# A fused attention, routed-expert and dense-layer kernel: the routed loop ahead of the last tile, the dense layer's operands in another order, its weights loaded four steps ahead

## The chip, the cores and the metric

One core of a Trainium2 chip runs the whole program. The metric is the device time of one execution in microseconds (us); the median over several executions counts. Engines are called by the names of the profile: PE multiplies matrices, DVE and ACT do elementwise work, POOL does elementwise work and the indexed transfers, SP issues nearly all other DMAs. Each engine takes its own instructions in the order in which the program lists them.

## What is computed

```python
attn_out = _attn_ref(q, k, v)            # windowed attention, 4 x 8 heads, 576 positions
x = attn_out.transpose(0, 2, 1, 3).reshape(2304, 512)
# routed experts: 8 experts, one for each token
h = np.maximum(x[mask] @ w1[e], 0.0)     # 512 -> 1024
out[mask] = gate_w[mask, None] * (h @ w2[e])
# dense layer, on all 2304 tokens
h = x @ w_in                             # 512 -> 2048
r = np.maximum(h, 0.0)
return ((r * r) @ w_out)                 # 2048 -> 512
```

## The kernel before

**Stages.** Attention fills the first 130 us or so. The tokens are then gathered by expert into five slots of up to 512 tokens (`NSLOT`, the last one of 384, `SHORT`), each with one expert: first the way up (8 products `ffn1`), then the way down, one tile of 128 tokens after the other (`ffn2`, 24 matrix products each). `put` copies a tile's result out of PSUM (L718) and `scatter` writes its rows to `yd` with an indexed DMA on POOL (L724). A loop (`tc.For_i`, L1100) takes further chunks of 128 tokens, as many as the routing asks for at run time; with these inputs its body does not run once. Then the dense layer takes the 2304 tokens in three blocks (`NB`) and four passes (`PASSES`), each pass with a quarter of the hidden width.

**Precision.** Every fp32 operand is held as a high part and a low part; ACT writes the high part (a cast), DVE or POOL subtracts it from the operand for the low part, and a product is three matrix products (`passes`, L688).

**The dense layer.** One pass on one block is a visit; there are twelve (`visits`). `way_up` has seven steps, n = 0 to 6, of two halves q with six matrix products each, by a scheme that multiplies sums and differences of quarter matrices: weights a11, s1, s2, a12, s3, s4, a22 against tokens b11, t1, t2, b21, t3, b22, t4. In steps 0 to 2 ACT copies each half out of PSUM (L1213); in steps 3 to 5 DVE adds the copy to the new half (L1216) and squares it (L1192), ACT casts (L1184) and POOL subtracts (L1185). Steps 0, 2, 4 and 6 use the same PSUM banks (tag s), so step 4 waits for the copies of step 2, and step 6 for the adds of step 4. `way_down` then makes six tiles. `prepare(j)` makes the seven token operands of a block: a difference (L1155, DVE), the high part (L1170, ACT), the low part (L1171; POOL for b21 and b22 of the later blocks, else DVE), and a store to `xs` for later passes. For the first block it runs within the first visit, for the others within the way down before.

**The dense weights.** They arrive as 64-bit floats. `conv` turns half a chunk into fp32 on ACT (L635), DVE (L636 to L639) and POOL (L640), and stores it to `wc` (L641); `conv_load` (L628) loads it. There are 32 such halves; `conv_pace` spreads them over all five slots. `weights(p)` makes the operands of pass p from `wc`: two loads (L783), seven splits (L788 on ACT, L789 on DVE), four sums (`both`, L794 on DVE), then two more chunks (L826, L827). It is a generator; each `tick()` advances it by one step. Pass 0's runs in the last slot, those of passes 1 to 3 in the last visit of the pass before.

**The end of the routed part.** The last tile of the last slot is not scattered and read back: its result `yhl` is added into the first block with a 0/1 matrix `hot` (L1063), in eight groups of products (L1296 and L688), while the other rows of the block are read from `yd` by `yload(0)` (L1011).

```python
for f in range(8):
    ffn2(ps, hs[f][0][:, c], hs[f][1][:, c], W[s, 4 + f // 2], f, f == 0, f == 7)
    ...
conv_step(len(convs) + 1)
flush(0)
while bg:
    tick()
...
with tc.For_i(4 * (NSLOT - 1), total, 1) as ci:
```

Of the kernel before, what the change touches and what calls it, by code (L numbers as in the profile page):

```python
# [52 lines left out]
def attention_moe_kernel(ctx, tc, qh, kh, v, mid, wg, mb, w1, w2, win, wout, out):  # L53
# [711 lines left out]
    nconv = [0]  # L765

    def conv_step(upto):
        while nconv[0] < upto:
            if nconv[0]:
                conv(*convs[nconv[0] - 1])  # L770
            if nconv[0] < len(convs):
# [8 lines left out]
    def weights(p):  # L780
# [23 lines left out]
        split("s1", s1)  # L804
        yield
        s2 = both(s1, a11, ALU.subtract)
        yield
        split("s2", s2)
        yield
        split("a12", a12)  # L810
        yield
        s3 = both(a11, a21, ALU.subtract)
# [3 lines left out]
        s4 = both(a12, s2, ALU.subtract)  # L816
        yield
        split("s4", s4)
        yield
        split("a22", a22)  # L820
        yield
        for i in range(2):
            r = load(2 * p + 8 + i)
            yield
            h, l = wt("left", F32R), wt("left", F32R)
            act.copy(h, r)  # L826
            dve.tensor_tensor(l, r, h.bitcast(F32), op=ALU.subtract)  # L827
            dw[p]["o", i] = h, l
            yield
# [190 lines left out]
    for s in range(NSLOT):  # L1020
        n, nn = (SHORT if i == NSLOT - 1 else SLOT for i in (s, s + 1))
        nxt = s + 1 < NSLOT
        for f in range(8 if s else 0):
# [14 lines left out]
            if not nxt:  # L1038
                tick()
# [14 lines left out]
        for i in range(n // 128):  # L1054
            advance_load(8 * s + 4 + i + LA + 1)
            c = slice(128 * i, 128 * i + 128)
            ps = bank("t")
            if not nxt and i == n // 128 - 1:
                ids, hot = sm.tile([128, 1], F32, tag="ids", name="ids", bufs=1), wt("left", F32R)
                dve.tensor_copy(ids, xr[s][0][:, i:i + 1])  # L1060
                dve.tensor_tensor(ids, ids, again, op=ALU.add)
                for k_ in range(BT):
                    dve.tensor_scalar(hot[:, 128 * k_:128 * k_ + 128], iota, 128.0 * k_, ids, op0=ALU.add, op1=ALU.is_equal)  # L1063
            for f in range(8):
# [3 lines left out]
                if f == 1 or f == 5:  # L1068
                    flush(1 if nxt or i < n // 128 - 1 else 0)
# [3 lines left out]
            if nxt or i < n // 128 - 1:  # L1073
                put(s, i, ps)
                if not nxt and i == n // 128 - 2:
                    yload(0)
            else:
                y, yhl = row(), wt("left", F32R)
                act.copy(yhl[:, :512], ps)
                dve.tensor_tensor(yhl[:, 512:], ps, yhl[:, :512].bitcast(F32), op=ALU.subtract)  # L1080
                act.copy(y, ps)
                ylast = s, i, y, yhl, hot
            if nxt or i < n // 128 - 1:
                advance_split(8 * s + 4 + i + LA + (0 if nxt else 1))

    conv_step(len(convs) + 1)
# [4 lines left out]
    for s in range(NSLOT):  # L1091
        if s < NSLOT - 1:
            del xr[s]
        for j in range(8):
            del W[s, j]
    p = ps = None
    hs.clear()
    held.append({})
    le, lo = (loop_int[:, i].rearrange("p a b -> p (a b)") for i in range(2))
    with tc.For_i(4 * (NSLOT - 1), total, 1) as ci:  # L1100
# [5 lines left out]
        xd_, hs = [x[0] for x in xT["d"]], []  # L1106
        for g in range(2):
            r, p = row(), bank("v", (128, 4, 128))
            for j in range(2):
                wload("d", expert_src(e, 2 * g + j))  # L1110
                wsplit("d")
                wh, wl = (w.rearrange("p (c f) -> p c f", c=4) for w in W["d"])
# [5 lines left out]
            hh, hl = (ht().rearrange("p (f t) -> p f t", f=4) for _ in range(2))  # L1118
            act.copy(hh, p)
            dve.tensor_tensor(hl, p, hh.bitcast(F32), op=ALU.subtract)  # L1120
            hs += [(hh[:, f, :], hl[:, f, :]) for f in range(4)]
        ps = bank("t")
        for f in range(8):
            if f % 2 == 0:
                wload("d", expert_src(e, 4 + f // 2))
                wsplit("d")
            ffn2(ps, *hs[f], W["d"], f, f == 0, f == 7)
        put("d", 0, ps)
        yload(0)
    held.clear()  # L1130
    xr.pop("d", None)
    xT.clear()
    W.pop("d", None)
# [16 lines left out]
    def prepare(j):  # L1150
# [7 lines left out]
        for n, o in enumerate(OPS):  # L1158
            if o == "t1":
                t[o] = minus(raw[0, 1], raw[0, 0])  # L1160
            elif o == "t2":
                t[o] = minus(raw[1, 1], t["t1"])
            elif o == "t3":
                t[o] = minus(raw[1, 1], raw[0, 1])
            elif o == "t4":
                t[o] = minus(raw[1, 0], t["t2"])
            else:
                t[o] = raw[int(o[1]) - 1, int(o[2]) - 1]
            x = operand(o)
            act.copy(x[:, 0], t[o])  # L1170
            (pool if n in (3, 5) and j else dve).tensor_tensor(x[:, 1], t[o], x[:, 0].bitcast(F32), op=ALU.subtract)  # L1171
            nc.sync.dma_start(out=xs[j][n], in_=x.bitcast(F32))
            yield
# [26 lines left out]
    def way_up(p, ahead, after):  # L1200
# [3 lines left out]
        for n, (o, wo, ps, first) in enumerate((("b11", "a11", a, True), ("t1", "s1", x, True), ("t2", "s2", a, False), ("b21", "a12", z, True), ("t3", "s3", a, False), ("b22", "s4", x, False), ("t4", "a22", a, False))):  # L1204
# [3 lines left out]
            for q in range(2):  # L1208
# [11 lines left out]
                tick()  # L1220
# [66 lines left out]
    s, i, y, yhl, hot = ylast  # L1287
    for h in range(2):
        for k in range(2):
            raw[k, h] = quarter()  # L1290
    for n, (k, h) in enumerate(((0, 0), (0, 1), (1, 1), (1, 0))):
# [7 lines left out]
    scatter(s, i, y)  # L1299
    del ylast, y, yhl, hot, xr[s], yr[0]  # L1300
# [3 lines left out]
    pre = prepare(0)  # L1304
    for _ in range(2):
        next(pre)
    for n_, (p, j) in enumerate(visits):
        fresh = visits[n_ + 1][1] if p == 0 and j + 1 < NB else None
        again_ = n_ + 1 < len(visits) and visits[n_ + 1][1] != j and fresh is None

        def ahead(n):
            if n_ == 0:
                next(pre, None)
# [5 lines left out]
        def after(n):  # L1319
            if again_:  # L1320
# [5 lines left out]
        if n_ == 0:  # L1326
            for _ in pre:
                pass
        between = lambda: None
        if fresh is not None:  # L1330
            turn_rows(fresh)
            pre = prepare(fresh)
            next(pre)

            def between():
                next(pre, None)

        way_down(j, p, between)
        if fresh is not None:
            for _ in pre:  # L1340
                pass
# [50 lines left out]
```

## Time and profile before

| | us |
|---|---|
| median of 3 executions (817.41 to 819.29) | 818.91 |
| the profiled execution, its own time | 822.86 |
| its span, first to last instruction | 821.2 |
| PE busy | 755.0 (92%) |
| DVE, ACT, POOL busy | 506.7, 343.3, 263.0 |
| mean granted TensorE clock, share of full | 0.962 |

The busy shares are means over unlike stages: attention, slots, the passage between the routed part and the dense layer, twelve visits. What counts is where PE, the busiest engine, stands still or runs at the lower of its two clock levels (0.50 in the rows, 1.2 of 2.4 GHz), and what it waits for there.

### The profile page before, as it was taken

To read this page: it belongs to the slowest core of one execution; us is meant where nothing else is said; L and a number is where in the kernel's file an instruction comes from. 1 tells how busy PE (TensorE), PEld (TensorE's weight loads), DVE (VectorE), ACT (ScalarE), POOL (GpSimd) and SP (SyncE) were. 2 spreads that over 40 slices of the span, in tenths; PEclk is the share of its full clock that TensorE was granted. 3 is DMA by queue.
4 is the path that set the end of the run, shared out by engine and by line. 5 is a ranking of instruction groups with operands and counts; after the bars stand their busy time and mean duration, and the time that the engine had idled before them with its cause. 6 is when DMAs were issued, how large, how long until landed. Compare 5 with 4: busy or idle time off the path is not lost.

```text
span 821.2 us, 12686 instructions
## 1 busy us (share of the span) xinstructions
PE 755.0 (92%) x4207; PEld 647.3 (79%) x4207; DVE 506.7 (62%) x1292; ACT 343.3 (42%) x833; POOL 263.0 (32%) x304
## 2 busy tenths in 40 slices
PE   9999887999999999991679996999989999899998
PEld 7777766778888888970678885889869899798996
DVE  7788879789768677794174437254283443843542
ACT  6677665236345454451256544423151132421321
POOL 4322355023633435231133412144040340422422
PEclk9999999999999999996789998999989999899999
DMA  8466340457877778744185582477625786166932
GB/s 268 159 231 227 119 146 34 145 178 286 305 271 233 273 249 288 277 141 153 66 306 240 183 346 104 154 319 303 242 83 204 283 341 241 67 238 237 365 125 77
DMA packets 71155, 174.72 MB, mean 213 GB/s; under 512 B 10032, under 2 KB 18480, under 8 KB 71088
## 3 DMA queue, kind: packets, MB, share of 16 engines
q1 hardware_dynamic: 68048, 163.93, 56.0%
q0 software_dynamic: 3040, 9.96, 3.1%
q8 instruction: 34, 0.56, 0.3%
q14 instruction: 33, 0.27, 0.1%
HBM read 117.76 MB, written 56.10 MB: 212 GB/s over the span
## 4 chain that ended last, share of the span: by engine, by line
PE 40%; DVE 5%; ACT 2%; DMA 2%; issue 2%; POOL 0%; SPq 0%; DVEq 0%; POOLq 0%; ACTq 0%
PE v L688 16%; PE t L688 10%; PE s L688 9%; PE m L688 2%; PE x L688 2%; DMA w<-wc 2%; DVE cr L1216 1%; DVE w L789 1%; DVE cr L1192 1%; DVE row L794 1%; ACT w L788 1%; ACT xq L1170 1%; DVE xq L1171 1%; DVE w L1155 1%; PE x L1296 0%
## 5 line engine op out<-in xcount | busy, mean ns | idle before, releaser
L1185 POOL TENSOR_TENSOR hd<-cr,hd 128x384 fp32r<-128x384 f32 x96 | 110.4, 1176 | 263.7 <-ACT hd L1184 241.9
L688 PE MATMUL v<-w,hd 128*128 128x512 f32 x576 | 141.1, 398 | 0.2 <-POOL hd L1185 0.2
L688 PE MATMUL s<-xq,w 128*128 128x384 f32 x576 | 115.4, 349 | 18.6 <-DVE cr L1216 10.9
L688 PEld LDWEIGHTS v<-w,hd 128*128 128x128 f32 x576 | 110.8, 193 | 23.6 <-POOL hd L1185 0.8
L688 PEld LDWEIGHTS s<-xq,w 128*128 128x128 f32 x576 | 105.2, 196 | 23.4 <-DVE cr L1216 8.9
L688 PE MATMUL t<-w,h 128*128 128x512 f32 x408 | 100.5, 399 | 1.8 <-ACT w L617 1.1
L688 PEld LDWEIGHTS t<-w,h 128*128 128x128 f32 x408 | 76.3, 191 | 18.4 <-ACT w L617 1.4
L640 POOL TENSOR_TENSOR row<-row 128x512 int32<-128x512 int32 x32 | 48.3, 1510 | 119.3 <-DVE row L639 84.7
L1184 ACT CAST hd<-cr 128x384 fp32r<-128x384 f32 x96 | 49.2, 513 | 70.1 <-DVE cr L1192 67.1
L1213 ACT COPY cr<-s 128x384 f32<-128x384 f32 x48 | 22.5, 479 | 131.2 <-PE s L688 131.2
L688 PE MATMUL t<-w,hd 128*128 128x512 f32 x288 | 69.2, 389 | 0.0
L688 PE MATMUL s<-w 128*128 128x512 f32 (+1 forms) x292 | 67.8, 384 | 1.1 <-DVE h L713 1.1
L1251 DVE SCALAR_TENSOR_TENSOR row<-v,gate,row 128x512 f32<-128x512 f32 x36 | 26.8, 749 | 65.6 <-PE v L688 63.7
L300 ACT ACTIVATE e<-x,m 128x128 f32<-128x128 f32 x128 | 50.3, 395 | 32.8 <-DVE m L279 32.8
L688 PEld LDWEIGHTS t<-w,hd 128*128 128x128 f32 x288 | 54.1, 188 | 11.3
L688 PEld LDWEIGHTS s<-w 128*128 128x128 f32 x292 | 53.3, 188 | 11.2 <-DVE h L713 2.0
L621 DVE TENSOR_TENSOR w<-w 128x1024 fp32r<-128x1024 f32 x37 | 49.4, 1339 | 17.8 <-ACT w L617 17.6
L1192 DVE SCALAR_TENSOR_TENSOR cr<-cr 128x384 f32<-128x384 f32 x72 | 54.7, 760 | 2.5
L1216 DVE TENSOR_TENSOR cr<-t,cr 128x384 f32<-128x384 f32 x24 | 13.3, 552 | 59.9 <-PE t L688 59.9
L339 POOL TENSOR_SCALAR_AFFINE_SELECT pt<-pt 128x512 f32<-128x512 f32 (+1 forms) x32 | 19.0, 593 | 84.4 <-ACT pt L335 65.5
L1171 DVE TENSOR_TENSOR xq<-w,xq 128x768 fp32r<-128x768 f32 x17 | 17.6, 1037 | 45.4 <-ACT xq L1170 45.4
L617 ACT CAST w<-w 128x1024 fp32r<-128x1024 f32 x37 | 38.7, 1048 | 1.8 <-DMA w<-w 1.6
(293 smaller groups left out, 1346.9 us busy)
## 6 DMA issues: line engine op xcount, KB each, us to landing
xq<-xs SPq DMA_DIRECT2D x42, 768.0 KB, 7.5
w<-w SPq DMA_DIRECT2D x40, 512.0 KB, 5.0
xs<-xq SPq DMA_DIRECT2D x21, 768.0 KB, 4.5
ya<-row SPq DMA_DIRECT2D x54, 256.0 KB, 2.1
row<-ya SPq DMA_DIRECT2D x54, 256.0 KB, 6.4
w<-win SPq DMA_DIRECT2D x16, 512.0 KB, 6.1
wc<-row SPq DMA_DIRECT2D x32, 256.0 KB, 2.6
w<-wout SPq DMA_DIRECT2D x16, 512.0 KB, 5.4
```

What stands on the lines that cost most here:

```text
L300: act.activation(e[:, i, j, :], x[:, i, j, :], AF.Exp, bias=m[:, i, j:j + 1], scale=-1.0, accum_out=rinv[b, t][:, h:h + 1])
L617: (dve.tensor_copy if quick else act.copy)(h, r)
L621: (eng or dve).tensor_tensor(l[:, c], r[:, c], h[:, c].bitcast(F32), op=ALU.subtract)
L640: pool.tensor_tensor(a, a, r, op=ALU.add)
L688: pe.matmul(ps, l, r, start=first and i == 0, stop=last and i == n - 1, **kw)
L1171: (pool if n in (3, 5) and j else dve).tensor_tensor(x[:, 1], t[o], x[:, 0].bitcast(F32), op=ALU.subtract)
L1184: act.copy(gh, c)
L1185: pool.tensor_tensor(gl, c, gh.bitcast(F32), op=ALU.subtract)
L1192: dve.scalar_tensor_tensor(c, c, 0.0, c, op0=ALU.max, op1=ALU.mult)
L1213: act.copy(c, ps[q])
L1216: dve.tensor_tensor(c, ps[q], c, op=ALU.add)
L1251: dve.scalar_tensor_tensor(o, ps, gate, o, op0=ALU.mult, op1=ALU.add)
```

## The change

Four parts. (1) 24 of the 32 weight conversions (`EARLY`) are paced over the slots; the other eight (`late_convs`, four in each of passes 1 and 2) become steps of the background generator in the dense layer; `conv` yields three times between its DVE instructions, so that one late half takes six ticks. The last slot ticks twice in each of its later ffn1 products and once in every second ffn2 step. (2) The loop stands before the last tile's `ffn2`, and `yload(0)` behind it. (3) `prepare` has 18 small steps in place of 7 large ones, makes differences some steps before the cast that reads them, starts within the eight groups for the first block, and has b21's and b22's low part on POOL for all blocks. (4) `weights` waits four steps between its first loads and their use, issues the loads of the last two chunks ahead, makes its sums on POOL, and starts earlier for passes 2 and 3; in passes 1 to 3 `way_up` ticks once a step.

```diff
+    EARLY, LATE = 24, 4
     def conv_pace(step):
-        conv_step(min(len(convs), max(0, step - 5) * len(convs) // 72) + 1)
+        conv_step(min(EARLY, max(0, step - 5) * EARLY // 59) + 1)
+    def late_convs(k):
+        for key, i in convs[k:k + LATE]:
+            conv_load(key, i)
+            yield
+            yield
+            yield from conv(key, i)
+            yield
+            flush(0)
...
         def both(a, b, op):
             t = row()
-            dve.tensor_tensor(t, a, b, op=op)
+            pool.tensor_tensor(t, a, b, op=op)
...
         top, low = load(2 * p), load(2 * p + 1)
+        yield
+        yield
+        yield
         yield
         a11, a12, a21, a22 = top[:, :512], top[:, 512:], low[:, :512], low[:, 512:]
         split("a11", a11)
-        yield
         s1 = both(a21, a22, ALU.add)
         yield
+        s3 = both(a11, a21, ALU.subtract)
         split("s1", s1)
         yield
         s2 = both(s1, a11, ALU.subtract)
-        yield
+        split("a12", a12)
+        yield
+        split("s3", s3)
+        yield
+        s4 = both(a12, s2, ALU.subtract)
         split("s2", s2)
         yield
...
+        r = [load(2 * p + 8 + i) for i in range(2)]
+        split("a22", a22)
...
             if not nxt:
-                tick()
+                tick(2 if f > 1 else 1)
...
+            if not nxt and i == n // 128 - 1:
+                break
...
-                if not nxt and f % 3 == 0:
+                if not nxt and f % 2 == 0:
                     tick()
...
     with tc.For_i(4 * (NSLOT - 1), total, 1) as ci:
...
-        yload(0)
     held.clear()
...
+    yload(0)
+    s, i = NSLOT - 1, SHORT // 128 - 1
...
+    for f in range(8):
+        ffn2(ps, hs[f][0][:, c], hs[f][1][:, c], W[s, 4 + f // 2], f, f == 0, f == 7)
+    y, yhl = row(), wt("left", F32R)
...
+        high("b11")
+        yield
+        low("b11", dve)
+        yield
+        make("t1", raw[0, 1], raw[0, 0])
+        yield
+        high("t1")
+        yield
+        make("t3", raw[1, 1], raw[0, 1])
+        yield
+        low("t1", dve)
+        yield
+        make("t2", raw[1, 1], t["t1"])
...
+        low("b21", pool)
...
-                tick()
+                if q or p == 0:
+                    tick()
...
+        step((2, 1, 3, 1)[n])
...
             if n_ == 0:
-                next(pre, None)
+                step((2, 3, 2, 2, 9, 0, 0)[n])
...
-        if n_ % NB == NB - 1 and p + 1 < PASSES:
+        if n_ % NB == (1 if p else 2) and p + 1 < PASSES:
             bg.append(weights(p + 1))
+        if n_ % NB == 0 and 0 < p < PASSES - 1:
+            bg.append(late_convs(EARLY + LATE * (p - 1)))
         way_up(p, ahead, after)
...
-            next(pre)
-
-            def between():
-                next(pre, None)
-
+            step(3)
+            between = lambda: step(3)
```

In the lists below an instruction has the line of its own version: the loop's L1100 is L1106 after the change, the products' L688 is L691. `wc_79` and `wc_80` are the chunks wc8 and wc9 of pass 0, `wc_84` to `wc_86` are wc13 to wc15.

**SP, where the slots end and the loop begins.** Before:

```order
L783 DMA w<-wc_79 128x1024
L628 DMA w<-wout 128x1024
L1011 DMA w<-yd 128x2x512 x3
L783 DMA w<-wc_80 128x1024
L641 DMA wc_85<-row 128x512
L641 DMA wc_86<-row 128x512 x2
L1100 COMPARE_AND_BRANCH
L1100 UNCONDITIONAL_BRANCH x2
```

After:

```order
L612 DMA w<-w 128x1024
L797 DMA w<-wc_79 128x1024
L797 DMA w<-wc_80 128x1024
L644 DMA wc_84<-row 128x512
L1106 COMPARE_AND_BRANCH
L1106 UNCONDITIONAL_BRANCH x2
```

The three loads from `yd` and the last stores to `wc` no longer stand ahead of the loop, and the loads of wc8 and wc9 no longer stand behind the loads from `yd`.

**DVE, from the loop's end into the first visit.** Before:

```order
L1100 UNCONDITIONAL_BRANCH
L1171 TENSOR_TENSOR xq<-w,xq 128x768
L1155 TENSOR_TENSOR w<-w 128x768
L1171 TENSOR_TENSOR xq<-w,xq 128x768
L1155 TENSOR_TENSOR w<-w 128x768
L1171 TENSOR_TENSOR xq<-w,xq 128x768 x2
L1155 TENSOR_TENSOR w<-w 128x768
L1171 TENSOR_TENSOR xq<-w,xq 128x768 x2
L1216 TENSOR_TENSOR cr<-t,cr 128x384
```

After (L1186 is the low part, L1173 the difference, L1266 the add):

```order
L1147 TENSOR_TENSOR w<-t,w 128x512
L1186 TENSOR_TENSOR xq<-w,xq 128x768
L1173 TENSOR_TENSOR w<-w 128x768 x2
L1186 TENSOR_TENSOR xq<-w,xq 128x768
L1173 TENSOR_TENSOR w<-w 128x768
L1186 TENSOR_TENSOR xq<-w,xq 128x768
L1173 TENSOR_TENSOR w<-w 128x768
L1186 TENSOR_TENSOR xq<-w,xq 128x768
L1266 TENSOR_TENSOR cr<-t,cr 128x384
```

Two low parts have left DVE, and the differences stand ahead of the low part that precedes their own cast.

**ACT, the way up of the last visit of pass 0.** Before:

```order
L1213 COPY cr<-s 128x384 x2
L788 CAST w<-w 128x512
L1213 COPY cr<-x 128x384
L1213 COPY cr<-m 128x384
L788 CAST w<-row 128x512
L1213 COPY cr<-s 128x384 x2
```

After (L1263 is the copy, L802 the split's cast):

```order
L1263 COPY cr<-s 128x384 x2
L1263 COPY cr<-x 128x384
L1263 COPY cr<-m 128x384
L1263 COPY cr<-s 128x384
L802 CAST w<-w 128x512
L1263 COPY cr<-s 128x384
```

The first cast that needs a loaded weight chunk now has one copy of steps 0 to 2 behind it, not four.

## Rows read from the trace of the kernel before

**Rows 1.** The page: busy time, share of the span and instructions of each engine.

```profile
PE 755.0 (92%) x4207; PEld 647.3 (79%) x4207; DVE 506.7 (62%) x1292; ACT 343.3 (42%) x833; POOL 263.0 (32%) x304
```

**Rows 2.** PE's waits, 395 to 821: engine, line, awaited: total us, times, longest us.

```profile
PE s L688 <- DVE cr L1216: 10.9, 7, 3.9
```

**Rows 3.** PE's timeline, 394 to 525: start, us, instruction [idle before <-releaser].

```profile
402.35 0.83 PE L1296 MATMUL v<-ident,w 128*128 128x128 f32 x6
...
403.38 0.83 PE L1296 MATMUL x<-ident,w 128*128 128x128 f32 x6
...
406.89 2.68 PE L688 MATMUL s<-xq,w 128*128 128x384 f32 x12 [1.30 <-ACT xq L1170]
...
449.58 2.27 PE L688 MATMUL s<-xq,w 128*128 128x384 f32 x12
...
484.64 2.27 PE L688 MATMUL s<-xq,w 128*128 128x384 f32 x12
...
498.50 3.94 PE L688 MATMUL s<-xq,w 128*128 128x384 f32 x12 [5.34 <-ACT cr L1213]
```

**Rows 4.** Timeline of all engines, 366 to 396, where the routed part ends.

```profile
376.28 1.40 SPq L1011 DMA_DIRECT2D w<-yd  x3
...
378.29 13.36 SPq L641 DMA_DIRECT2D wc<-row  x3
385.34 1.04 ACT L826 CAST w<-w 128x1024 fp32r<-128x1024 f32 x1 [15.67 <-DMA w<-wc]
...
390.05 1.25 POOL L640 TENSOR_TENSOR row<-row 128x512 int32<-128x512 int32 x1 [15.65 <-DVE row L639]
...
395.00 1.22 PE L1296 MATMUL x<-ident,w 128*128 128x128 f32 x4 [23.25 <-SPq L1100]
```

**Rows 5.** Stretches: length, busy PE, PEld, DVE, ACT, POOL, PE clock, DMA share, GB/s.

```profile
355.00:358.00 3.00, 1.17 (x5) 0.54 (x4) 2.77 (x4) 2.98 (x6) 0.63 (x1) 1.00 0.53 146
358.00:366.30 8.30, 8.30 (x30) 6.51 (x31) 7.30 (x14) 3.35 (x6) 1.67 (x1) 0.79 0.39 123
499.00:501.00 2.00, 2.00 (x8) 2.00 (x7) 1.31 (x3) 1.14 (x2) 0.00 (x0) 0.50 0.00 0
525.30:556.20 30.90, 30.90 (x157) 28.08 (x156) 11.96 (x19) 8.35 (x17) 9.36 (x8) 1.00 0.75 281
587.20:625.40 38.20, 34.69 (x158) 30.36 (x157) 23.52 (x33) 13.30 (x25) 8.70 (x8) 0.91 0.37 138
687.30:724.40 37.10, 34.26 (x158) 30.30 (x157) 23.59 (x33) 13.31 (x25) 8.72 (x8) 0.91 0.39 142
```

**Rows 6.** Groups by line and shape: busy us, mean ns of one, idle before.

```profile
L1192 DVE SCALAR_TENSOR_TENSOR cr<-cr 128x384 f32<-128x384 f32 x72 | 54.7, 760 | 2.5
...
L640 POOL TENSOR_TENSOR row<-row 128x512 int32<-128x512 int32 x32 | 48.3, 1510 | 119.3 <-DVE row L639 84.7 <-issue 24.7 <-PE s L688 4.6
...
L794 DVE TENSOR_TENSOR row<-w 128x512 f32<-128x512 f32 x8 | 5.5, 684 | 0.0
```

**Rows 7.** The page, DMA issues: queue, times, KB each, median us to landing.

```profile
w<-win SPq DMA_DIRECT2D x16, 512.0 KB, 6.1
wc<-row SPq DMA_DIRECT2D x32, 256.0 KB, 2.6
```

**Rows 8.** DMA issues, 355 to 400, with the same columns.

```profile
w<-yd SPq DMA_DIRECT2D x3, 512.0 KB, 4.5
...
yd<-row,idx POOLq DMA_INDIRECT x3, 3.3
```

**Rows 9.** Timeline, 405 to 432: a DVE instruction alone, and one beside POOL.

```profile
407.75 0.95 DVE L1155 TENSOR_TENSOR w<-w 128x768 f32<-128x768 f32 x1
...
420.69 1.28 POOL L1185 TENSOR_TENSOR hd<-cr,hd 128x384 fp32r<-128x384 f32 x1 [23.97 <-ACT hd L1184]
421.03 1.76 DVE L1155 TENSOR_TENSOR w<-w 128x768 f32<-128x768 f32 x1
```

**Rows 10.** ACT's timeline, 478 to 525: the first cast of pass 1's weights.

```profile
495.47 0.62 ACT L788 CAST w<-w 128x512 fp32r<-128x512 f32 x1 [7.99 <-DMA w<-wc]
```

More of the change, by code (lines that the diff above doesn't have):

```diff
@@ L769, in conv_step @@
             if nconv[0]:
-                conv(*convs[nconv[0] - 1])
-            if nconv[0] < len(convs):
+                for _ in conv(*convs[nconv[0] - 1]):
+                    pass
+            if nconv[0] < EARLY:
                 conv_load(*convs[nconv[0]])
@@ L1089, in attention_moe_kernel @@
         tick()
-    for s in range(NSLOT):
-        if s < NSLOT - 1:
-            del xr[s]
+    for s in range(NSLOT - 1):
+        del xr[s]
         for j in range(8):
@@ L1096, in attention_moe_kernel, with chunk @@
     p = ps = None
-    hs.clear()
     held.append({})
+    def chunk(src):
+        r, h, l = (take(("w", dt), n, lambda: wpools["right"].tile([128, 1024], dt, tag="w", name="w")) for dt, n in ((F32, 2), (F32R, 4), (F32R, 4)))
+        nc.sync.dma_start(out=r, in_=src)
+        act.copy(h, r)
+        dve.tensor_tensor(l, r, h.bitcast(F32), op=ALU.subtract)
+        return h, l
     le, lo = (loop_int[:, i].rearrange("p a b -> p (a b)") for i in range(2))
@@ L1124, in attention_moe_kernel @@
             if f % 2 == 0:
-                wload("d", expert_src(e, 4 + f // 2))
-                wsplit("d")
-            ffn2(ps, *hs[f], W["d"], f, f == 0, f == 7)
+                w = chunk(expert_src(e, 4 + f // 2))
+            ffn2(ps, *hd_[f], w, f, f == 0, f == 7)
         put("d", 0, ps)
-        yload(0)
     held.clear()
-    xr.pop("d", None)
-    xT.clear()
-    W.pop("d", None)
+    del xr["d"], xT["d"]
+    yload(0)
+    s, i = NSLOT - 1, SHORT // 128 - 1
+    ids, hot = sm.tile([128, 1], F32, tag="ids", name="ids", bufs=1), wt("left", F32R)
+    dve.tensor_copy(ids, xr[s][0][:, i:i + 1])
+    dve.tensor_tensor(ids, ids, again, op=ALU.add)
+    for k_ in range(BT):
+        dve.tensor_scalar(hot[:, 128 * k_:128 * k_ + 128], iota, 128.0 * k_, ids, op0=ALU.add, op1=ALU.is_equal)
+    ps, c = bank("t"), slice(128 * i, 128 * i + 128)
+    for f in range(8):
+        ffn2(ps, hs[f][0][:, c], hs[f][1][:, c], W[s, 4 + f // 2], f, f == 0, f == 7)
+    y, yhl = row(), wt("left", F32R)
+    act.copy(yhl[:, :512], ps)
+    dve.tensor_tensor(yhl[:, 512:], ps, yhl[:, :512].bitcast(F32), op=ALU.subtract)
+    act.copy(y, ps)
+    scatter(s, i, y)
+    W.clear()
+    hs.clear()
     experts.close()
@@ L1156, in minus, with make, high, low @@
             return d
[L1158 to L1167, printed above, removed]
-                t[o] = raw[int(o[1]) - 1, int(o[2]) - 1]
[L1169 to L1173, printed above, removed]
+        def make(o, a, b):
+            t[o] = minus(a, b)
+        def high(o):
+            if o not in t:
+                t[o] = raw[int(o[1]) - 1, int(o[2]) - 1]
+            act.copy(operand(o)[:, 0], t[o])
+        def low(o, eng):
+            x = xo[o]
+            eng.tensor_tensor(x[:, 1], t[o], x[:, 0].bitcast(F32), op=ALU.subtract)
+            nc.sync.dma_start(out=xs[j][OPS.index(o)], in_=x.bitcast(F32))
+        high("b11")
[7 more added lines that the diff above has]
+        make("t3", raw[1, 1], raw[0, 1])
+        yield
+        low("t1", dve)
+        yield
+        make("t2", raw[1, 1], t["t1"])
+        yield
+        high("t2")
+        yield
+        low("t2", dve)
+        yield
+        make("t4", raw[1, 0], t["t2"])
+        yield
+        high("b21")
+        yield
+        low("b21", pool)
+        yield
+        high("t3")
+        yield
+        low("t3", dve)
+        yield
+        high("b22")
+        yield
+        low("b22", pool)
+        yield
+        high("t4")
+        yield
+        low("t4", dve)
         raw.clear()
@@ L1285, in way_down, with step @@
         gs.clear()
-    s, i, y, yhl, hot = ylast
+    def step(n):
+        for _ in range(n):
+            next(pre, None)
     for h in range(2):
@@ L1332, in attention_moe_kernel @@
             pre = prepare(fresh)
-            next(pre)
-            def between():
-                next(pre, None)
+            step(3)
+            between = lambda: step(3)
         way_down(j, p, between)
         if fresh is not None:
-            for _ in pre:
-                pass
+            step(9)
         if n_ % NB == NB - 1:
```

59 lines of the change are left out of this document (16 added, 43 removed).

## The prediction

> **What bounds the kernel now.** PE does: it is busy for 755 of 821 us [rows 1]. So I looked for the time in which it is not, in three views. First PE's waits and its own timeline: in the dense layer PE stands still for DVE's adds, 10.9 us in seven waits [rows 2], and once for 5.34 us for ACT's copies [rows 3]. Second the timeline of all engines around the longest wait, a hole of 23.25 us that ends at 395.0 [rows 4]. Third the stretches: an undisturbed visit takes 30.9 us with PE busy for all of them, while the last visits of passes 1 and 2 take 38.2 and 37.1 us at a mean clock of 0.91 [rows 5]. The visits of pass 0, by their first products, take 42.7, 35.1 and 40.7 us [rows 3, 5]. The second is the clean measure for the first, since both have 24 transposes ahead of their way down, which later ones lack; the third has none of them and should take 30.9.
>
> **The change, part by part.** The sum is made against the profiled execution, 822.86 us (span 821.2 and 1.7 around it). The median of the runs shown is 4.0 us less; I take that off at the end.
>
> *Slot 4.* From 355 to 358 PE is busy for 1.17 of 3.00 us while DVE is busy for 2.77; then PE runs for 8.3 us at a mean clock of 0.79 [rows 5]. That is 1.8 us idle, and with 0.42 of the time at half clock another 0.42 x 8.3 / 2 = 1.7 us. The change takes some six conversions out of this slot, each with four DVE instructions of 128x512 at 0.7 us or less by L794 [rows 6], and four sums; the pass-0 splits stay, only closer together. I take 3.1 us gained; bounds 0 and 3.5.
>
> *The hole.* SP must first read `yd`, which waits for the scatter of the tile before the last and starts at 376.28, then load wc9, then store three conversions. ACT's cast of wc9 heads ACT's queue for 15.67 us; behind it wait the multiply of the last conversion (so its DVE part, POOL at 390.05, the store at 391.3) and the eviction of the last tile. PE starts at 395.0, released by the loop [rows 4]. A store takes 2.6 us to land [rows 7], so the loop itself costs about 395.0 - 391.3 - 2.6 = 1.1 us.
>
> After the change none of that stands ahead of the loop. What does is the scatter of the tile before the last: about 1.1 us for its copy out of PSUM (half of L826's 1.04 us) and the handing over to POOL, 3.3 us from issue to landing [rows 8], 1.1 for the loop: 5.5 us in which PE idles. Then the last tile runs. After 5.34 us of idleness PE's clock is 0.50, and twelve products take 3.94 us, not 2.27 [rows 3, 5]; for the tile I add 1.9 us. Another 0.7 us passes until its high and low part are there for the groups. Sum 8.1. The three reads by `yload(0)` take 1.40 us to issue and 4.5 to land [rows 4, 8], 5.9 in all; the tile takes 7.3 (24 products; a way down has 72 in 30.9 less seven steps of 2.1, so 24 take 5.4, and 1.9 for the clock). They are hidden, not by much. What goes is 23.3 us, and 2.4 in the groups, which took 10.6 us to 405.6 where eight at their later spacing of 1.03 take 8.2 [rows 3]. Gain 25.7 - 8.1 = **17.6 us**; bounds 13 (the reads late) and 19 (the clock kept).
>
> *The first visit.* Its first product waits 1.30 us for b11 [rows 3]; after the change cast and low part run beside the groups. Gain 1.3. The visit itself takes 42.7 us against 35.1. Before, DVE makes difference and low part in turn and waits for ACT between them; after, three differences and two low parts come before the visit, and one difference and three low parts, 0.95 us each by L1155 [rows 9], are spread over it, with two low parts on POOL. I leave 0.9 us of delay, since b21's store now waits for POOL on SP, and the read of the next block (`yload`) is queued behind it, some 5 us into a way up of 14.6. Gain 6.7; bounds 4 and 7.6.
>
> *The last visit of pass 0.* It loses 9.7 us. The 5.34 us wait is ACT, standing at the cast of a11 until 495.47, 10.8 us into the visit, with four copies of steps 1 and 2 behind it [rows 3, 10]. After, one copy is behind it. The loads stand where they stood in the program; only their use is later. The last store ahead of them comes a step of the way down earlier, so I let them land after 9.3 us. From there DVE has in turn, at 0.7 us for a 128x512 [rows 6], the low parts of a11 and s1 (the latter after POOL's sum and ACT's cast, to 12.1 us), two adds and squares at 0.5 + 0.76 [rows 6], two more low parts, and the add for which step 6 waits: 16.6 us, where PE wants it after 12.5. With the rest of that chain and some half clock I leave 6.1 us lost. Gain 3.6; bounds 0 and 9.
>
> *The last visits of passes 1 and 2.* They lose 7.3 and 6.2 us, with DVE busy for 23.5 us, not 12.0 [rows 5]. After, the generator starts in visit 1, its first loads land in a way down, and of its low parts only five fall into the last way up, two of them in steps 3 to 5. I leave 0.6 us in each. Gain 12.3; bounds 5 and 13.5.
>
> *The late conversions.* Eight times 2.7 us of DVE at most, 1.5 of POOL [rows 6] and 768 KB [rows 7], in visits where DVE is busy for 12 of 30.9 us and DMA at 0.75 [rows 5]: PE hides them. I allow 0.2 us in each of four visits, 0.8. Without that cover they cost 22 us.
>
> *Sums on POOL.* A sum takes 0.68 us on DVE [rows 6]. On POOL it lies between L640's 1.51 us [rows 6] and L1185's 1.28 x 512/384 = 1.7 [rows 9]; I take 1.55, nearer the same shape. At the ends of passes 1 and 2 three of four fall into a way down, where both engines have room. One thing speaks against the move. L1155 takes 0.95 us alone, and 1.76 us where it starts 0.34 us into a POOL subtraction of 1.28: about what is left of that, and then its own time [rows 9]. The Trainium skill ("SBUF — State Buffer", "Who interferes with whom") says that a DVE instruction with two SBUF inputs and a POOL instruction that reads SBUF exclude each other, the later one waiting for the whole of the other; the trace agrees here. By that rule a moved sum can cost DVE more than it saves: the second rival.
>
> Sum: 3.1 + 17.6 + 1.3 + 6.7 + 3.6 + 12.3 - 0.8 = 43.8 us. 822.9 - 43.8 = 779.1 for an execution like the profiled one; less 4.0, **775.1 us**.
>
> **The rivals.** (1) *The last visit of pass 0 becomes clean as well*: its loads land before ACT reaches the cast, by 5.3 us. For it: the store ahead of them moves up. Against: all stores of the block are still ahead. Gain 9 for 3.6: 770.
>
> (2) *POOL holds DVE up where DVE is last.* If each sum blocks DVE for all its 1.55 us, it costs 0.87 us more than before: 3.5 us in the last visit of pass 0, the 3.1 us of slot 4, and for the two wider low parts of the first visit 2 x 0.87 x 768/512 = 2.6. 775.1 + 9.2 = 784. Rows 9 speak for it; against it that POOL is free most of the time and few instructions overlap.
>
> (3) *The weights' load on DVE only moves*, and two visits a pass lose half each of what one lost. The 12.3 us are gone: 787. Against: with DVE at 12 of 30.9 us PE loses nothing.
>
> (4) *The loop still ends late*, by a DMA that it drains or a read that I time wrongly: half to all of the 17.6 us, 784 to 793.
>
> (5) *Slower: ACT at the late conversions' loads.* Each L635 comes two ticks after its load, 2.7 to 4.2 us, and such a load takes 6.1 us [rows 7]. ACT would stand there with copies behind it, as in the last visit of pass 0, which lost 9.7 us. From the fifth of eight such stalls on the 43.8 us are used up (5 x 9.7 = 48.5): 824, and 853 if all eight stall. Against: of four halves in a pass only the first has copies of steps 0 to 2 near it, and in the way down of passes 1 and 2 PE waits for nothing of ACT's.
>
> **How the numbers follow.** The forecast, within some 5 us, has a chance of 0.46; rival 1 0.15, rival 2 0.19, rival 3 0.08, rival 4 0.08, rival 5 0.04. The range takes in rivals 1 to 3 with the bounds around the forecast and the near half of rival 4: 765 to 791. A measurement tells about 0.2%, 1.6 us, from no change. All cases but rival 5 lie well below 818.9: faster 0.95, slower 0.04, and 0.01 for a balance.
>
> **What would show it.** Right: one PE wait of 5 to 6 us at the loop and the last tile behind it; a first visit of 35 to 37 us; last visits of passes 1 and 2 under 32; no PE wait for ACT's copies in visits with late conversions. Wrong: a hole over 10 us at the loop, ACT waiting for `win` or `wout` in steps 0 to 2, or a last visit of pass 0 still over 39 us (then the load sets it, not DVE).

## The result and the profile after

The changed kernel takes **792.03 us** (median of 4 runs, 790.08 to 795.78) where the kernel before, in the same session, takes 818.72: a ratio of 0.9682, 95% interval 0.9642 to 0.9722. Faster, as forecast, but by 26.7 us and not by 43.8: the time lies 17 us above the forecast and 1 us above the range. (By its time alone it would fit rival 4, 784 to 793, but the loop does not end late.)

The page answers to [rows 1]: PE has lost 10 us of busy time, POOL has gained 38.

```profile
PE   744.9 (94%) x4207; PEld 636.0 (81%) x4207; DVE 504.0 (64%) x1274; ACT 342.6 (43%) x833; POOL 300.8 (38%) x322
```

```profile
PE s L691 <- DVE cr L1266: 6.2, 3, 4.7
PE t L691 <- DVE ids L1138: 5.6, 1, 5.6
```

Those are two of PE's waits over the whole run (total, times, longest). The first answers to [rows 2]: three waits are left of seven. The second is the loop.

The timeline of all engines at the loop answers to [rows 4]:

```profile
360.75 0.97 POOL L727 DMA_INDIRECT yd<-row,idx  x1 [3.73 <-POOLq L1106]
364.74 1.59 SPq L1025 DMA_DIRECT2D w<-yd  x3
...
365.41 7.35 PE L691 MATMUL t<-w,h 128*128 128x512 f32 x24 [5.55 <-DVE ids L1138]
...
372.60 0.83 PE L1351 MATMUL x<-ident,w 128*128 128x128 f32 x6
```

The scatter lands some 3.4 us after its issue at 360.75, SP is past the loop at 364.74, and PE idles for 5.55 us, not 23.25. The tile takes 7.3 us, and the groups start without a wait.

The stretches, with the columns of [rows 5]. Of before: slot 4 to the first visit, the first visit, the last visit of pass 0.

```profile
334.50:406.90 72.40, 46.02 (x234) 41.17 (x232) 39.81 (x64) 25.48 (x43) 16.86 (x16) 0.81 0.43 149
406.90:449.60 42.70, 37.87 (x181) 32.81 (x182) 26.77 (x33) 22.80 (x45) 12.60 (x10) 0.92 0.68 261
...
484.60:525.30 40.70, 33.81 (x158) 29.45 (x158) 20.21 (x28) 17.75 (x32) 9.66 (x9) 0.92 0.43 162
```

Of after: the same stretch, then the visits of passes 0 (first and last), 1 and 2.

```profile
331.70:381.60 49.90, 44.05 (x234) 39.41 (x234) 27.50 (x39) 22.07 (x37) 15.21 (x14) 0.93 0.40 146
381.60:419.30 37.70, 34.92 (x181) 30.44 (x180) 23.99 (x29) 23.17 (x46) 18.28 (x12) 1.00 0.71 274
...
454.40:496.60 42.20, 34.89 (x158) 30.62 (x157) 19.61 (x24) 17.41 (x31) 15.16 (x12) 0.88 0.40 155
496.60:529.70 33.10, 31.83 (x158) 27.84 (x157) 17.50 (x27) 9.72 (x19) 12.14 (x10) 1.00 0.84 299
529.70:563.10 33.40, 31.47 (x157) 27.93 (x156) 18.60 (x29) 9.62 (x20) 14.40 (x12) 1.00 0.92 344
563.10:594.80 31.70, 31.43 (x157) 27.97 (x156) 21.26 (x28) 12.24 (x24) 15.67 (x11) 1.00 0.38 138
594.80:627.40 32.60, 31.89 (x158) 27.88 (x157) 18.26 (x28) 9.01 (x18) 12.16 (x10) 1.00 0.85 304
627.40:659.70 32.30, 31.43 (x157) 27.92 (x156) 18.17 (x29) 9.26 (x19) 12.84 (x11) 1.00 0.95 349
659.70:691.40 31.70, 31.40 (x157) 27.95 (x157) 21.96 (x29) 12.38 (x24) 17.22 (x12) 1.00 0.40 144
```

The last visits of passes 1 and 2 are cured (31.7 for 38.2 and 37.1). The last visit of pass 0 is 1.5 us longer than before. And the four visits with late conversions, 30.95 us each before, now take 33.13, 33.45, 32.56 and 32.36 (from their first products): 7.7 us.

Two stretches ask for a cause. In the last visit of pass 0 (from 454.40; all engines):

```profile
458.10 3.87 SPq L797 DMA_DIRECT2D w<-wc  x4
464.70 0.62 ACT L802 CAST w<-w 128x512 fp32r<-128x512 f32 x1 [4.34 <-DMA w<-wc]
466.06 2.54 POOL L808 TENSOR_TENSOR row<-w 128x512 f32<-128x512 f32 x2 [12.10 <-DMA w<-wc]
...
473.24 0.54 DVE L1266 TENSOR_TENSOR cr<-s,cr 128x384 f32<-128x384 f32 x1
473.84 2.29 PE L691 MATMUL s<-xq,w 128*128 128x384 f32 x6 [4.67 <-DVE cr L1266]
```

The cast of a11 starts 10.3 us into the visit, and the add for which step 6 waits starts at 18.8 and ends at 19.4. The visit is 11.3 us over a clean one of 30.9: PE idles for 7.3 (42.2 less 34.9 busy), and its mean clock of 0.88 costs the other 4.0 (34.9 less 30.9). In the second visit of pass 1 (from 529.69):

```profile
537.23 0.44 SPq L628 DMA_DIRECT2D w<-win  x1
...
545.38 0.43 DVE L636 TENSOR_SCALAR row<-w 128x512 int32<-128x512 int32 x1 [3.32 <-DMA w<-win]
545.47 0.67 ACT L635 ACTIVATE row<-w 128x512 f32<-128x512 f32 x1 [4.15 <-DMA w<-win]
...
546.60 0.74 PE L691 MATMUL v<-w,hd 128*128 128x512 f32 x2 [1.46 <-ACT hd L1234]
```

DVE and ACT stand at the heads of their queues for a load, with a step's add and a cast behind it. From the issue of this load to its first use 8.2 us pass, the longest of the eight; the others take 4.7 to 7.2.

### The profile page after: what moved, and what is told of

Its sections match the earlier page's. It is cut to its first block, busy times and chain, and to the rows that moved or that the text cites. A ratio compares the mean times of both kernels' runs of the same rounds, so it can differ in the third digit from the quotient of the medians.

```text
span 788.4 us, 12648 instructions
## 1 busy us (share of the span) xinstructions
PE 744.9 (94%) x4207; PEld 636.0 (81%) x4207; DVE 504.0 (64%) x1274; ACT 342.6 (43%) x833; POOL 300.8 (38%) x322
## 4 chain that ended last, share of the span: by engine, by line
PE 39%; DMA 5%; DVE 4%; issue 3%; POOL 2%; ACT 1%; SPq 0%; POOLq 0%; DVEq 0%; ACTq 0%
PE v L691 14%; PE t L691 10%; PE s L691 9%; PE x L691 2%; PE m L691 2%; DMA w<-wout 2%; DMA w<-win 1%; DVE cr L1242 1%; POOL row L643 1%; DVE cr L1266 1%; DMA w<-wc 1%; POOL hd L1235 1%; DVE w L803 1%; DMA yd<-row,idx 0%; DMA wc<-row 0%
## 5 line engine op out<-in xcount | busy, mean ns | idle before, releaser
L1235 POOL TENSOR_TENSOR hd<-cr,hd 128x384 fp32r<-128x384 f32 x96 | 119.1, 1267 | 144.8 <-ACT hd L1234 137.3
L691 PE MATMUL v<-w,hd 128*128 128x512 f32 x576 | 141.3, 395 | 5.3 <-POOL hd L1235 2.7
L691 PEld LDWEIGHTS v<-w,hd 128*128 128x128 f32 x576 | 107.9, 189 | 32.0 <-POOL hd L1235 6.1
L691 PE MATMUL s<-xq,w 128*128 128x384 f32 x576 | 111.1, 340 | 8.0 <-DVE cr L1266 6.2
L691 PEld LDWEIGHTS s<-xq,w 128*128 128x128 f32 x576 | 102.2, 191 | 11.0 <-DVE cr L1266 7.0
L691 PE MATMUL t<-w,h 128*128 128x512 f32 x408 | 100.6, 400 | 5.6 <-DVE ids L1138 5.6
L691 PEld LDWEIGHTS t<-w,h 128*128 128x128 f32 x408 | 76.3, 191 | 22.2 <-issue 6.0
L691 PE MATMUL t<-w,hd 128*128 128x512 f32 x288 | 69.2, 389 | 0.0
L691 PE MATMUL s<-w 128*128 128x512 f32 (+1 forms) x292 | 67.9, 384 | 1.1 <-DVE h L716 1.1
L691 PEld LDWEIGHTS t<-w,hd 128*128 128x128 f32 x288 | 54.1, 188 | 11.3
L691 PEld LDWEIGHTS s<-w 128*128 128x128 f32 x292 | 53.3, 188 | 11.3 <-DVE h L716 2.0
L621 DVE TENSOR_TENSOR w<-w 128x1024 fp32r<-128x1024 f32 x37 | 50.0, 1356 | 17.7 <-ACT w L617 17.2
L1263 ACT COPY cr<-s 128x384 f32<-128x384 f32 x48 | 22.6, 479 | 73.4 <-PE s L691 73.4
L1242 DVE SCALAR_TENSOR_TENSOR cr<-cr 128x384 f32<-128x384 f32 x72 | 51.8, 720 | 2.5
L636 DVE TENSOR_SCALAR row<-w 128x512 int32<-128x512 int32 x32 | 13.7, 428 | 46.4 <-DMA w<-win 22.2
L617 ACT CAST w<-w 128x1024 fp32r<-128x1024 f32 x37 | 38.6, 1047 | 2.9 <-DMA w<-w 2.9
L635 ACT ACTIVATE row<-w 128x512 f32<-128x512 f32 x32 | 21.5, 671 | 41.0 <-DMA w<-win 19.4
```

Source lines behind the costliest of these rows:

```text
L617: (dve.tensor_copy if quick else act.copy)(h, r)
L621: (eng or dve).tensor_tensor(l[:, c], r[:, c], h[:, c].bitcast(F32), op=ALU.subtract)
L691: pe.matmul(ps, l, r, start=first and i == 0, stop=last and i == n - 1, **kw)
L1235: pool.tensor_tensor(gl, c, gh.bitcast(F32), op=ALU.subtract)
L1242: dve.scalar_tensor_tensor(c, c, 0.0, c, op0=ALU.max, op1=ALU.mult)
L1263: act.copy(c, ps[q])
```

## The experiments

Twelve variants of the changed kernel ran. A time is the median of four executions, for the last four variants of two; a row or a visit is read from one profiled execution. Where an edit adds or removes lines, line numbers are shifted by a few. "The stretch" is the time from the first product of slot 4 to that of the first visit: 72.36 us before, 49.84 after, but 50.7 to 50.8 in the three runs below whose code is the same up to there (late conversions one half ahead, early first weights, block 0's low parts): the last tile took 7.35 us in after and 8.35 in the first of them, so about 1 us of after's gain is one execution's.

**Late conversions loaded one half ahead.**

```diff
-        for key, i in convs[k:k + LATE]:
-            conv_load(key, i)
+        some = convs[k:k + LATE]
+        for n, (key, i) in enumerate(some):
+            if n + 1 < LATE:
+                conv_load(*some[n + 1])
...
+        if n_ % NB == NB - 1 and p < PASSES - 2:
+            conv_load(*convs[EARLY + LATE * p])
```

> Each half of the late conversions is loaded one half ahead of its use, the first one in the way down of the visit before; nothing else moves. Theory A (ACT and DVE stand at the head of their queues for the load): the two visits with late conversions in pass 1, 33.13 and 33.45 us, and in pass 2, 32.56 and 32.36 us, fall to 31.0 to 31.6 each, 5.5 to 7.5 us in all, so about 785.5 us by the median. Theory B (the extra work on DVE and POOL and their exclusion of each other lengthen these visits): each stays within 0.5 us of what it was, 791 to 792.

787.88 us, ratio 0.9599 (0.9566 to 0.9632). The four visits take 32.31, 30.94, 32.31 and 30.95: 5.0 of the 7.7 us are gone, and the second visits are entirely clean. Theory A for two thirds. What is left sits in the first visits; there:

```profile
509.95 2.68 POOL L1237 TENSOR_TENSOR hd<-cr,hd 128x384 fp32r<-128x384 f32 x2 [19.14 <-ACT hd L1236]
510.25 1.50 DVE L638 SCALAR_TENSOR_TENSOR row<-w,row 128x512 int32<-128x512 int32 x1
...
513.73 2.69 POOL L1237 TENSOR_TENSOR hd<-cr,hd 128x384 fp32r<-128x384 f32 x2 [1.09 <-PE m L691]
514.03 1.50 DVE L640 SCALAR_TENSOR_TENSOR row<-row 128x512 int32<-128x512 int32 x1
...
517.45 1.31 POOL L1237 TENSOR_TENSOR hd<-cr,hd 128x384 fp32r<-128x384 f32 x1 [1.04 <-ACT hd L1236]
517.81 1.24 DVE L642 TENSOR_SCALAR row<-w 128x512 int32<-128x512 int32 x1
...
521.62 1.88 PE L691 MATMUL v<-w,hd 128*128 128x512 f32 x7 [0.78 <-POOL hd L1237]
```

Three of DVE's four conversion instructions start 0.3 us into a low part of POOL's and take 1.50, 1.50 and 1.24 us, where alone they take 0.69, 0.69 and 0.42; each delays the adds, so POOL's later low parts, for which PE waits 0.78 us here. That this is all of the 2.7 us left in the two first visits is argued from the durations, not shown by a run.

**No late conversions.**

```diff
-    EARLY, LATE = 24, 4
+    EARLY, LATE = 32, 4
...
-        for key, i in convs[k:k + LATE]:
...
+        for _ in range(6 * LATE):
+            yield
```

> All 32 halves are converted in the slots again, at the change's faster pace, and none in passes 1 and 2; the ticks stay, so the weights' loads stand where they were. The four visits must fall to 31.0 to 31.2 us whatever their cause, 7.5 us in all. Open is what the slots and the loop pay. Theory A (the hole at the loop came from ACT standing at wc9, which the change's later use cures): the hole stays under 9 us and the slots pay 2 to 6 us, 787 to 791. Theory B (it came from the conversions' stores ahead of the loop): the hole is back at 15 us or more, over 795.

787.40 us, ratio 0.9597 (0.9568 to 0.9626). The four visits take 30.94 or 30.95, and the stretch 50.94: the hole is 5.62 us, slot 4 no slower. Theory A's hole and time came true; its price for the slots of 2 to 6 us is not seen. Slot 4 starts at 335.62 here, at 333.97 and 336.23 in the two runs of everything together, which have the same code up to there, and at 333.5 to 334.9 in the six with late conversions below: 1 us on average, no more than such runs differ by. As the change loads them, the late conversions were taken out of a place where they cost less than where they went; loaded one half ahead they cost the same (787.88 and 787.40 us).

**Pass 1's first weights loaded before the way down of the second visit.**

```diff
-        top, low = load(2 * p), load(2 * p + 1)
+        top, low = first or (wc_load(2 * p), wc_load(2 * p + 1))
...
+        if n_ == 1:
+            first = wc_load(2), wc_load(3)
```

> The first two loads of pass 1's weights are issued before the way down of the second visit of pass 0, ahead of the block's stores; the splits and sums stay in their ticks. Theory A (the load's landing, 10.3 us into the last visit of pass 0, sets that visit): it falls from 42.16 us to 34 to 36.5, and the time to 785 to 787. Theory B (the sums on POOL and the low parts that they hold up set it): it stays over 40 us, and the time over 790.

787.02 us, ratio 0.9592 (0.9561 to 0.9623). The visit falls from 42.16 to 34.72 us: theory A.

```profile
464.95 0.62 ACT L803 CAST w<-w 128x512 fp32r<-128x512 f32 x1
...
474.73 1.31 PE L691 MATMUL s<-xq,w 128*128 128x384 f32 x6 [1.83 <-DVE cr L1267]
```

The visit starts at 459.10; the cast of a11 comes at its tick, 5.9 us in, and PE's wait for step 6 is 1.83 us, not 4.67. The profiled execution as a whole is no shorter than that of after (790.64 and 790.08 us): its first visit takes 38.74 us and the second visits of passes 1 and 2 take 34.62 and 34.91, all three at a mean clock of 0.95 or 0.96 where after has 1.00. That is not this edit: the last run below, without it, has 35.11 for such a visit. By medians the edit gains 5.0 us.

**The sums back on DVE.**

```diff
-            pool.tensor_tensor(t, a, b, op=op)
+            dve.tensor_tensor(t, a, b, op=op)
```

> The four sums of each pass go back to DVE, nothing else. Theory A (the landing sets the last visit of pass 0): it stays at 41 to 43 us; the time is 791 to 794. Theory B (POOL's sums, and DVE's low parts that wait for them and beside them, set it): it falls under 39.5 us, and the time to 789 or less.

792.15 us, ratio 0.9659 (0.9626 to 0.9692); the last visit of pass 0 takes 40.44. It lies just under theory A's bounds and above B's: the landing sets the visit, and the sums on POOL cost 1.7 us of it, some 2 by all profiles: with sums on POOL and the load late, the visit takes 42.2 to 43.0 us in six profiles, with sums on DVE 40.2 to 40.4 in four. The time is that of after all the same.

**Block 0's low parts of b21 and b22 on DVE.**

```diff
-        low("b21", pool)
+        low("b21", pool if j else dve)
...
-        low("b22", pool)
+        low("b22", pool if j else dve)
```

> The two low parts that the change gives to POOL for the first visit (b21, b22) go back to DVE for block 0; nothing else. In the run without late conversions a square of DVE that started 0.34 us into such a POOL low part took 1.93 us where its like takes 0.56, and a low part beside the second 1.44 where its like takes 0.95. Theory A (POOL holds DVE up in the first visit): the visit falls from 37.7 us to 36.0 to 36.8, since DVE has gaps of 0.9 to 1.5 us there for its own two parts of 0.95. Theory B (DVE has too much work in that visit): it stays at 37.4 or grows to 39.5.

794.06 us, ratio 0.9677 (0.9657 to 0.9697). The first visit takes 38.53 us, at a mean clock of 0.96 where that of after has 1.00. At that clock it takes 38.74 without the edit (the run with early first weights); with the edit and the clock kept it takes 37.42 (the two runs of everything together, below), for 37.72 in after. So the edit is worth 0.2 or 0.3 us; theory A fails, and B holds. In the changed kernel the square does pay:

```profile
389.31 1.85 POOL L1186 TENSOR_TENSOR xq<-w,xq 128x768 fp32r<-128x768 f32 x1 [1.93 <-ACT xq L1182]
389.65 1.92 DVE L1242 SCALAR_TENSOR_TENSOR cr<-cr 128x384 f32<-128x384 f32 x1
```

but two parts of 0.96 us on DVE cost nearly as much. The visit stays 2.6 us above the second one, and the profile of after tells where: 1.9 us of them PE stands idle. In the first visit it waits 2.3 us for DVE's adds and squares at the end of the way up (the three rows below; L1245 is step 6's square and L1282 a transpose behind it), in the second 0.4. DVE is busy for 24.0 us in the first and 17.7 in the second. That this load is the whole reason is argued: no run takes more of it away.

```profile
PE s L1282 <- DVE cr L1245: 1.0, 2, 0.6
PE s L691 <- DVE cr L1266: 0.7, 1, 0.7
PE m L1282 <- DVE cr L1266: 0.6, 1, 0.6
```

**The last tile's products back ahead of the loop.** (The twelve lines from `ids, hot = ...` to `act.copy(y, ps)` move up, ahead of `held.append({})`.)

> The last tile's products go back ahead of the loop, as before the change; the conversions and the weights stay as the change has them, and the scatter of that tile stays behind the loop. Theory A (the tile behind the loop hides the reads of yd, as predicted): PE gets through the loop some 5.5 to 7 us later than after the change but has the tile done, then waits 4 to 6 us for the reads: the first visit starts within 2 us of 385. Theory B (the hole came from the conversions at the heads of the queues alone, and the scatter that the loop waits for is hidden by the tile just as well): no wait over 3 us, first visit 3 to 6 us earlier, 379 to 382. Theory C (the loop waits for the tile's eviction and for the reads in turn): first visit 3 us or more later.

794.49 us, ratio 0.9687 (0.9655 to 0.9719). The stretch is 50.91 us, no longer than elsewhere:

```profile
369.39 0.59 ACT L1103 COPY row<-t 128x512 f32<-128x512 f32 x1 [0.76 <-DVE w L1102]
370.22 2.33 SPq L1025 DMA_DIRECT2D w<-yd  x3
...
374.11 2.03 PE L1353 MATMUL x<-ident,w 128*128 128x128 f32 x6 [6.10 <-DMA w<-yd]
```

Theory A: the loop lets go when ACT's last eviction is done, and PE then waits 6.10 us for the reads. Behind the loop the tile hides the reads, ahead of it the scatter. In this kernel moving it is worth nothing: the stretch is within 0.3 us of the three runs named above, and the time within the interval of after's.

**All of it together**: no late conversions, early loads with the first split three steps sooner (`for _ in range(1 if first else 4): yield`), low parts on DVE; then the same with the sums on DVE.

> Together: all conversions in the slots, the first loads of pass 1's weights ahead of the stores of the visit before, with the first split three steps sooner, and block 0's low parts on DVE; sums on POOL. If the causes add up: first visit 36 to 37 us, last visit of pass 0 32 to 34, visits of passes 1 and 2 at 31.0 but the last at 31.7; 777 to 780 us. If the early loads cost elsewhere what they gain: 783 or more.

> As the run before it, with the four sums of each pass on DVE. Theory A (with the loads early, POOL has time, and the sums no longer bind): within 1.0 us of the other in the last visit of pass 0, and up to 0.7 us more in the last visits of passes 1 and 2. Theory B (a sum on POOL costs DVE more than it saves wherever they overlap): the last visit of pass 0 is 1.0 to 2 us shorter.

**776.01 us**, ratio 0.9464 (0.9442 to 0.9486), and 777.57, ratio 0.9466 (0.9444 to 0.9488). Visit by visit the causes add up: against after the twelve visits are 17.2 us shorter, and the time is 16.0 us less. Of that 2.0 us is the sooner split, which was not tried alone (34.72 to 32.72 in the last visit of pass 0). By medians the three edits alone gave 4.6, 5.0 and -2.0 us, 7.6 in all, so the sum holds by visits only; the executions of one kernel lie 1 to 6 us apart. The first visit misses its expectation, 37.42 for 36 to 37. The other visits are the clean ones expected; the last of pass 0, then pass 1's three:

```profile
456.80:489.50 32.70, 31.84 (x157) 27.82 (x156) 17.78 (x24) 17.21 (x31) 15.99 (x12) 1.00 0.44 167
489.50:520.50 31.00, 31.00 (x158) 28.12 (x157) 11.95 (x19) 8.36 (x17) 9.34 (x8) 1.00 0.73 280
520.50:551.40 30.90, 30.90 (x157) 28.08 (x156) 14.16 (x22) 9.44 (x19) 13.35 (x11) 1.00 0.80 314
551.40:583.40 32.00, 31.71 (x158) 27.93 (x157) 19.77 (x27) 11.54 (x22) 13.12 (x10) 1.00 0.37 133
```

With the sums on DVE the last visit of pass 0 takes 33.70, 1.0 us more: theory A. With the loads early, POOL is the better place in this visit; the two times are not told apart.

**What made the hole.** A ladder back to the kernel before, each step on top of the last: `weights` with its ticks in the last slot, and the pace of the conversions, as before (no late ones); the tile ahead; the reads of `yd` ahead. And the reads alone on the changed kernel. Of the edits only the pace and the place of the reads are shown here.

```diff
-        conv_step(min(EARLY, max(0, step - 5) * EARLY // 59) + 1)
+        conv_step(min(EARLY, max(0, step - 5) * EARLY // 72) + 1)
...
+            if not nxt and i == n // 128 - 2:
+                yload(0)
```

> No late conversions; all 32 halves at the pace of before, and pass 0's weights split and summed as before (sums on DVE, one tick after the load, each of the last two loads cast in the next tick). The tile and the reads of yd stay behind the loop. Read is the stretch from the first product of slot 4 to the first of the first visit: 72.4 us before, 49.9 after the change, 51.0 with all conversions in the slots at the new pace. Theory A (ACT at the head of its queue for the weights' load, and the conversions behind it): 62 us or more. Theory B (the reads of yd ahead of the loop hold SP, so that the weights' load and the stores come late): 51 to 56. The visits of passes 1 to 3 say nothing on it.

> As the run before it, and the last tile's products ahead of the loop again; the reads of yd stay behind it. Theory A: 62 us or more in the same stretch. Theory B: within 3 us of the run before it.

> As the run before it, and the reads of yd ahead of the last tile again: now all that the change did ahead of the loop is undone. The stretch must be back at 70 us or more by every theory, less what the change gains in the groups and at b11 (some 3 us).

> The changed kernel with one thing undone: the reads of yd stand ahead of the loop, behind the last tile but one. Theory B, for a kernel with one store behind the reads and no weights' load: SP is held for the scatter, 5 to 6 us, and the stretch is 49 to 54 us, so the reads alone do no harm. If it is 58 or more, the reads' place alone made most of the hole.

The stretch: 50.94 with no late conversions, then **65.52**, 68.61, 69.43 (before: 72.36; the 2.9 us left are what the change gains in the groups and at b11, as expected); and **58.07** with the reads alone. (797.15, 799.98, 801.08 and 803.22 us.) By the time theory A holds: weights and pace, which were not tried apart, make 14.6 us, some 2 of them in slot 4 (below) and the rest at the loop. The tile's place, worth nothing on the changed kernel, makes 3.1 here. The reads' place, worth 0.8 at the end of the ladder, costs 7 to 8 alone; by the letter of its expectation (58 or more) it made most of the hole, though 7 to 8 are a third of the 21.5 in all. The first step of the ladder:

```profile
366.52 9.04 SPq L644 DMA_DIRECT2D wc<-row  x3
...
373.95 1.25 POOL L643 TENSOR_TENSOR row<-row 128x512 int32<-128x512 int32 x1 [1.18 <-DVE row L642]
...
375.65 0.37 SPq L792 DMA_DIRECT2D w<-wc  x1
379.32 1.04 ACT L835 CAST w<-w 128x1024 fp32r<-128x1024 f32 x1 [10.53 <-SPq L1101]
380.40 1.22 DVE L836 TENSOR_TENSOR w<-w 128x1024 fp32r<-128x1024 f32 x1 [6.53 <-ACTq L1101]
381.98 1.58 SPq L1020 DMA_DIRECT2D w<-yd  x3
```

and the reads alone:

```profile
366.06 1.40 SPq L1025 DMA_DIRECT2D w<-yd  x3
367.51 0.46 SPq L644 DMA_DIRECT2D wc<-row  x1
374.82 0.09 POOL L726 MEMSET spacer<- 1x1 f32 x1 [11.16 <-SPq L1108]
```

In both the loop ends when the last thing issued ahead of it is done: a low part of the last weights at 381.6, a store that lands 6.6 us after 367.51. Each brake holds the loop by itself, and they do not add; the change took both away.

The mechanism of theory A is not what the first step shows. In the kernel before, the last conversion does stand behind ACT's cast of wc9 [rows 4]. Here it does not: its ACT part runs at 368.11 and its POOL part ends at 375.2. It is the load of wc9 that stands, on SP, behind the conversions' stores, which hold SP for 9.04 us. So stores ahead of a load on one queue, and a cast ahead of a conversion on another, lead to the same late end.

## Why the prediction was wrong

In the frame of the profiled executions the change was to give 43.8 us. By its terms it gave 30.3:

- *Slot 4, the hole, b11*: 3.1 + 17.6 + 1.3 = 22.0 predicted, 72.36 - 49.84 = **22.5** measured. Right in size, and in the 5.5 us that stay at the loop; about 1 us of it is one execution's (above). The story was right in what stood ahead of the loop. But slot 4's term came for another reason: PE's two waits there, 1.1 us for ACT (L617) and 0.8 for DVE (L621), are gone with all conversions in the slots too, and back with the old weights and pace. And the tile, which the working credits with hiding the reads, hides a scatter just as long elsewhere.
- *The first visit*: 6.7 predicted, **5.0** measured, within its bounds. The working leaves 0.9 us of delay over the second visit and puts it to SP; it is 2.6, and 1.9 of them are longer waits of PE for DVE.
- *The last visit of pass 0*: 3.6 predicted, **-1.5** measured; outside the bounds 0 to 9. Two steps failed. "I let them land after 9.3 us": the cast started after 10.3, for 10.8 before. The stores ahead of the loads held SP until 458.05, 3.7 us into the visit, for 4.2 before, and the cast comes 6.6 us behind the first issue in both; with the loads ahead of the stores the visit is 7.4 us shorter. And the chain from there to the end of the add was 9.1 us, where the working has 7.3: the sums on POOL, which cost 1.7 us or a little more here, half of what rival 2 gives them. In all the visit loses 11.3 us, where the working leaves 6.1: 2.8 by these two steps, and the rest behind that add and by the clock, which costs 4.0. The forecast's own sign, "then the load sets it, not DVE", has come true.
- *The last visits of passes 1 and 2*: 12.3 predicted, **12.0** measured.
- *The late conversions*: 0.8 predicted, **7.7** measured. The failed step is "PE hides them": it weighed the engines' busy time and not the order of their queues. Rival 5 named this wait and the two ticks' lead. It came, though what cost PE time behind it was adds and casts of later steps: copies of step 0 stood behind it too, in the second visit of pass 1, where ACT waits until 532.46, and cost PE nothing. From 496 to 690 DVE waits at seven of the eight loads, 40.1 us in all (14.4 of them ahead of the first add of the first visit, where it has no other work), and PE loses 1.4 to 2.5 us a visit, not 9.7 a stall. Told only as a way to be slower, it had a chance of 0.04; at a small price it belonged in the sum. Loading earlier removes 5.0.
- *Less 4.0*: a profiled execution that is 4.1 us above its median was read as if every term were as large in the others. By profiles the gain is 32.8 us, of which 2.8 lie ahead of slot 4 and are chance (last section); by medians it is 26.7. 822.86 - 30.3 = 792.6 is nearly the median of after, so hardly any of the 4.0 came back. That before was slow in the very waits that the change removed would explain it; of the seven executions of before in the first experiments the shortest (817.39) has a mean clock of 0.974 and the longest (822.18) one of 0.963, the profiled one 0.962. Only one execution of it was profiled, so this stays open.

Together 13.5 us of terms and 3.5 of the frame: the 17 us.

## What to carry to other kernels

Work is not hidden by an idle engine, but by an idle engine whose queue does not stand: before moving a conversion beside other work, put its load as far ahead of its use as the load takes there (4.7 to 8.2 us here, the longest with the DMA engines 0.9 busy), and count what stands behind it on each queue. In every trace here the loop with an unknown count ended only when what was issued ahead of it was done: a scatter, an eviction, a low part, a store. Look at the last transfer and the last queue head ahead of it before moving compute across it. And price a rival's mechanism apart from its sign: a wait that would need a great price to turn the result can still take a sixth of the gain.

## What the runs showed that was not expected

- The exclusion of DVE and POOL reaches an instruction with one input in SBUF: L642 takes 1.24 us for 0.42 when it starts 0.36 us into a low part of POOL's. The Trainium skill ("SBUF — State Buffer", "Who interferes with whom") puts the operation of this kind (tensor_scalar) among those that can take the shared ports when their operands meet its conditions, which no run here varies; the trace agrees in that this one is held up.
- A wait far ahead of the change differs between runs of the same code. PE's wait for the reciprocal L390, some 120 us into the run, is 0.3 us in the profiled run of after (first row) and 2.7 in all twelve variants and in before (second row, before):

```profile
PE v L478 <- DVE ri L390: 0.3, 1, 0.3
```

```profile
PE v L478 <- DVE ri L390: 2.7, 1, 2.7
```

Of the 2.8 us by which after's slot 4 started earlier than before's, 2.4 are this one wait; and with the wait at 2.7 slot 4 starts anywhere from 332.9 to 336.2 in the variants. A difference of that size between two profiled executions says nothing of a change.
